# Plain float32 in the second feed-forward product, decays and state sum in one instruction each, and another order

## The chip, the cores and the metric

The kernel runs on one core of one Trainium2 chip. The metric is device time in microseconds (us) of one execution. The engines are PE (TensorE: matmuls, with its weight loads shown as PEld), DVE (VectorE), ACT (ScalarE), POOL (GpSimd) and SP (SyncE), which only issues transfers here. Each engine works through its own instructions in order; semaphores tie the engines to each other.

## The reference

Three layers, one after the other, all in float32.

```python
for t in range(S):                      # B, H, S, D = 4, 8, 768, 40
    y[:, :, t] = r_t @ state
    Sa = state @ a_t
    state = state * w_t - outer(Sa, b_t) + outer(v_t, k_t)
x = y.transpose(0, 2, 1, 3).reshape(B, S, 320)

h = relu(x @ w_in)                      # 320 -> 1024
conv = sum(conv_w[k] * h shifted by k - 1 tokens for k in 0, 1, 2)
x = (h * sigmoid(conv)) @ w_out         # 1024 -> 320

# four causal attention heads of 64 as experts, the best two of four mixed per token
```

The first layer is a recurrence over 768 tokens. The second is the feed-forward part; `w_out` is its second product. The third is attention over each of the four sequences.

## The kernel before, in words

**Recurrence.** The 768 tokens are cut into NT = 12 steps of 64, each into NC = 2 chunks of 32. `prep(n)` builds for a step what doesn't need the state: running products of the decays w (P) and their inverses (Q), k and b times Q (L297), a times P (L301), small products of the two (L313), a triangular inverse T. `chain(k)` carries the state from chunk to chunk: X (L448), the solved part (L464), the state's change as 16 products (L477), the sum with the old state (L496) and its decay (L498). `post(k)` gives the outputs y, multiplies by P (L549) and writes them to a scratch in memory.

The tile `a` holds two heads, in partitions 0 to 39 and 64 to 103, and two places for each. `load_a` puts head 0 into place 0 and head 1 into place 1; the free rows (64 to 95 of place 0, 0 to 31 of place 1) later receive F, the masked products of a and k (L319, L323). So the decays times a are two instructions of 40 partitions x 1024, one for each place (L299 to L302).

The 16 products of L477 fill the first 320 columns of two PSUM banks, four blocks of 80 in each. The state sum is therefore one instruction for each bank (L490 to L496).

**Feed-forward.** `ff()` makes one stage for each step and each of four pairs of 128-row blocks of h: 48 stages, and two more for what lags (LAG = 2). A stage does 16 first products (L683, 8 passes x 2 blocks), takes h out of PSUM (L693), and `gate` works it on: two ACT copies times conv_w (L645), four DVE instructions for the other taps (L649), the sigmoid (L652), times h on POOL (L654). Then the result g is split in two: `gh`, rounded to the fp32r format (L657, ACT), and `gl`, what is left (L660, POOL). Two stages later the second product takes them (L714): for each of two blocks and two halves of 128 tokens three fp32r products, gh x wh, gh x wl, gl x wh. The weights w_out are split in the same way at the start (L606 to L608). The last token is a small product of its own at the end (L728 to L733). `cv`, `h`, `gh` and `gl` have two buffers each, the loaded input `xd` one.

**Attention.** `proj`, `weigh`, `scale`, `turn`, `values` and `result` work through blocks of 128 queries; plain float32 products appear there in `values` (L944), and transposes in `turn` (L921).

**Order.** The parts are generators, merged by due times into one program. `in_order` then reads the table ORDER: for each engine a text of pairs (skip, size), each of which takes the next instructions of that engine, `size` of them, after `skip` of those still left. So the order on every engine is written out in full, and the engine waits wherever the next instruction in this order is not ready.

Of the kernel before, what the change touches and what calls it, by code (L numbers as in the profile page):

```python
# [8 lines left out]
F32 = mybir.dt.float32  # L9
# [34 lines left out]
def paced(g, start, span):  # L44

    for f in g:
# [11 lines left out]
        "Wg0k8A04-0C4kg04-0y4-0i8-0K8-1e80w-1y4-0a4-1u6M8wg08og0oAg-0UgY4w4Y2U4-2y6U8-2ii0Ego-1i40M-0y4k4-2G4g40A88I804"
        "8w0444cgYg04-0y4gg-0i8-2ma-0i8-264-2a2-264-0i40-02-1240gk80gA8-3644w04-2y6sg4gQg4w-1i204-1240w-0y40g8g-02444sw"
        "g8w88404Ygc4k4048804-0-4-0W404-0Ok-164-0O4-2S408gwwo-1S4wg-1C2wg0w8w-0s40g-064-084-062sg-2e404-2a6-0S4-1-40gMg"  # L60
        "-1y2-1u40w-0i8-128-0S40M4g8404cwk4sg-0egc8-0S4-0O4sg-0u4-0C4-0uc-2me-0K4-0eE-0K804-1u604-0C404-0yg-3O4-1240w-3"
        "e8-12g0w-2i80w-1O48g0wQ40wM8E40g4gU8-26agw04k4-1u2c4MgogUg0484-0q404-0m4-2ya04-0i8-2m2-0i4-2a8-0C8-168-0y4-1S4"
        "-4mc0w-0Cg-1Cg-3m40w-2S2-024-2U80w-4A4-2i40w-1O2-3-48g0wQ40wM8-0m8E40g-0244g04cw04ggogMg-0C4-0qc-2i404-0m4-06g"
        "04-02k-1mk0ww8-028-3Sc-06g0wQg0w-2q4-2mc4g-26g04-283-2e3-223g4-2130w48A84w-1f404-0M4-0P44gkg04-0f40k-0340g-034"
        "0wx4F8Zg-0j8-0r8-0D4-0L803-0I464033e09j30c76fc-22307gco4wco2r7o308scgai4g2w3g6m408ec8g082g062407O30gs3X3cc3394"
        "09M3cc03940c9g09e2-1A2kg0bo407-0P20624-1V2j8225cU805s3048g08cg-0r40cOc04K423056304240k430ch83b6402h401g4348432"
        "06a302m40143a404a36433d3v303a4y3a4w3a482e8C3g2I3e204C3ac04u7g604o3a202g8A408G2v8N3y4m30gv3630423023403C425x475"
        "02ec0594e80994g492i405d8944504u8egt80594k609l452j4548404134201ak34024401640376c4340854eo540554a4d40553c352h4q4"
        "0553i458rga4f8w2f405ncw40554y254Jkj8a605q4j4b8h4u408m2c393v4j406l4d4037343g304y344-003c488-04608aoq2a4w2a4s124"
        "s306e484a8j3850863z8h3t3063403w3c408m404g20cA248V40465Acr404a524s3o4068508g35404120184l8Ck845309m8540554e254i4"  # L70
        "t4055e05kci205ik04450454a805g456f405a4fo05r4j4a4j205a4d4g405io5305n6346406320j7k047234843172028405dg0514d61364"
        "420192gc021202h434d202130314012802240e",
    "Activation":
        "-0Z1-1m1110131012104a1l111411104f1j101110331514101219151312101f15161g1012111a11103210272e1g1f111d1a10111b1a1w1"
        "1101g101l102f111j1e1f1e101m111g1i2o211j1m1l102h111i1h1g1h1k1g21101h1e301l1d202k1h211g1b1a1g1037281731171i46101"
        "7111013342311161b1049101c11151c111b1a10111014201b1d1b2310122c101110181s1c1511121110112025122311101211141312111"
        "612161114321117121011101c13101310142g1i101g1f13101e101b1221101110151016172c1917201a1032103f2b2a2r192p404120181"
        "f121118101b101e1n241m1n1m10162a121b1a1018101d13101510141617101i161B16181e1110221028402q13103i1l1j181h221118102"
        "a10192211101k101j1i1h101h1v1g12251610151m15141G10171i1110211410421c184o4026131011101f1g12111013101211102l102n1"
        "41g10112610161e1a151a13181n1317132j11204d1b1d1c1b1r10112314131210131m11202c15101b131025261e1014111b29101218101"  # L80
        "6111b28101814171042101l101f2e10121e1c20411315111k1110181h42103410141211101713141813181g131e18171u161b4a2716142"
        "j1h161310141d1w101e151c101a104m11202m121f1116102b1t1b24101419102614281a1e1910171b101628101o17181410151n151g1h4"
        "g1w16102t11201q1r1q13103110111C201217101110161a1n1e10131210232g13181e28161b16171018151m101620151f151f2u1f10212"
        "a201k1A1k102112111f2p1f111e11201j1k101k1i101s1h2120131j1311201r1g101f1j1h1f1h1f1h1i2j1i1o1k1n2u30261E1D1610151"
        "815102513151310121720151810141726101a2937101a1619471015181517101a1614152013161015121522131210111h10122521161a1"
        "2112f101e1220121112141310121011291410131610121312101b1011131712161210161011141A101413101s101E12202f12102715112"
        "01C131413102214111210221110411021102622211316102411121023191310111015141214121015101115161112181228221011181j1"
        "3161015162b151029101a1815103a171011102314101911121011132013102210131220251l15132620241210141113202311121310221"
        "1101210131112101225131013111215101125121413161015161i151a1210111b24121316101316131c171510151410361510111213111"
        "0171b121e11101c101d13401410142013142312151011131029111416101510131110141013101f1210111011181617131710321316101"  # L90
        "214121025182130141113141210141011121d1110151415141014201113101210111320132013141310141015201710111012104110121"
        "0111312102420111413102520211410211011107",
    "DVE":
        "0821112111211121112111511131211101j211i2m1o1n1o1n1r102l11101m101m101g1l101i101h101h101g10as101-00141Z101Y102W1"
        "n1V1X12101U1l1T1l1W1V1Y1X1-011-001-011-00112011101k101j1n1j1m101F101k108310a113111211202v102w131c2m1f1j1i131h1"
        "0121011101p1o103p101p101n102r101q1B1q1A1q1j1s111r111q111p101o2r5u1r1t1r1s1r1u1r2310121011101l1w401v101v101u1t1"
        "u1t1u1t1i1s2012101m111i102l1g2i1g101g101g1f11102b101c201b1018102610151014121c12101513101210211011101p20g412131"
        "6121510161410454815101514a91514163215121810112024101413301211203k101j101i201h105d102510121012102a1810262011202"
        "g101f101l102j111n12101210121012101120151032101q102o1r2m111011101t101h101o101n101m1l103e104a1019106n102l10112w1"
        "11m102k101211121112111211121115111312111A121110221q1u1q101n103k11101p107k101j101g101f1075101310211l101k1153121"  # L100
        "31211841211201c151t131s132q131p1051107f207c10261015101410161022131011402m10121k1311131113111311151115111312112"
        "0111018101210211011108i101h102f101e101d102410131021103810171012201112113o1210121012101210121012101112112012111"
        "01a101110211p1n1s221112111k111i1110ae10551c1014101310271620112i111h111n111311131h141114111411171115102d1015102"
        "11011102110111j101i101h101g101i101h301g101g109910161716102n102l1s121r10111u111N1110131013102G10111011101110141"
        "0121043102n101m111011101l207e101d101c101c1039101810171016104h22201e2013102i101h3l202j23105j1h1i1h101l1j1k1j102"
        "6201518151025132012161j162h16101f101617162h1019101f1e3617161c1b101519151c15101435101410122312201610241210111c1"
        "610151418221011101a1013111023111211101g3311121310211m112u102b1I2G1H151G1F131j1D101i101h1110131112111t502210111"
        "021103435212023152032101c12102610171e171d151c141612161g1210171d101c12151c111b2811171211151a3f111e20241f1c1e1c4"
        "61b541c341c1027141610311025121415141013111019111617212210111a11121017201c3311102m1n1m10141k341j121i321h2410131"
        "11014321310121015323024321026321012111c30111321101115121b112924231n131o1n101m1l381510141h111g271f171e171119231"  # L110
        "017121320281612161512202916141012152f14101d27101f1a1e2t3c2011101c2a1v1b1a20191q191p19221822161217121022151i121"
# [32 lines left out]
class Kernel:  # L144
# [1027 lines left out]
```

## Time and profile before

| | us |
|---|---|
| median of 3 runs | 866.12 (865.93 to 870.81) |
| the profiled execution | 866.72 |
| its span, first to last instruction | 864.9 |
| PE busy | 726.0 (84%) |
| DVE busy | 681.5 (79%) |
| ACT busy | 576.8 (67%) |
| POOL busy | 370.2 (43%) |
| mean granted clock of PE | 0.931 |

Busy times are unions: two matmuls that lie over each other count once, and a matmul's record is longer than the time until the next may start. The recurrence ends near 525 us, the feed-forward part near 632, and attention runs from about 540 to the end. Shares of the whole span mix these stretches, so the rows below are taken by stretch or by line.

### The profile page before, as it was taken

The page shows a single profiled execution, that of the slowest core. Times are in us where ns is not written, and L with a number is a line of the kernel's source. Part 1 is how long each engine was busy: PE and PEld are TensorE (multiplying, and loading weights), DVE is VectorE, ACT ScalarE, POOL GpSimd, SP SyncE. Part 2 cuts the span into 40 slices and gives each one's busy share as a digit, 9 for nine tenths or more (in the row PEclk, how much of TensorE's full clock was granted, in tenths as well). Part 3 has the DMA queues.
Part 4 walks back from the last instruction along what each step waited for, and adds up shares of the span by engine and source line. Part 5 has one row for each costly group of instructions (what it writes and reads, how often), then busy time and mean ns, then how long its engine had stood idle before and what let it go on. Part 6 is the DMA issues. An engine that isn't in the chain of part 4 may idle for free. (4 is left out here: it accounts for less than half of the span.)

```text
span 864.9 us, 31373 instructions
## 1 busy us (share of the span) xinstructions
PE 726.0 (84%) x13080; PEld 639.9 (74%) x13080; DVE 681.5 (79%) x1541; ACT 576.8 (67%) x1359; POOL 370.2 (43%) x419
## 2 busy tenths in 40 slices
PE   1366658989978998988898897888999999999997
PEld 1255547878877877877797786887888888888876
DVE  6996968899989999999979854776667776877764
ACT  1274747677675785866676885689777665676665
POOL 6233463524424233153143437567543454442652
PEclk9997568599999897997979999999999999999999
DMA  5445576556656556565645444301010101110001
GB/s 134 109 114 134 139 162 157 119 111 158 141 137 134 130 120 129 134 126 132 152 101 144 109 100 127 87 20 30 16 50 36 48 16 33 38 39 17 16 17 39
DMA packets 143488, 81.17 MB, mean 94 GB/s; under 512 B 113858, under 2 KB 127042, under 8 KB 142386
## 3 DMA queue, kind: packets, MB, share of 16 engines
q1 hardware_dynamic: 138450, 74.34, 35.7%
q0 software_dynamic: 4896, 4.83, 2.7%
q8 instruction: 103, 1.69, 0.8%
q14 instruction: 39, 0.32, 0.1%
HBM read 51.63 MB, written 11.80 MB: 73 GB/s over the span
## 5 line engine op out<-in xcount | busy, mean ns | idle before, releaser
L907 POOL TENSOR_TENSOR A<-A,rs 128x128 f32<-128x128 f32 (+5 forms) x96 | 88.5, 943 | 102.1 <-DVE rs L905 79.3
L649 DVE SCALAR_TENSOR_TENSOR cv<-h,cw,cv 128x256 f32<-128x256 f32 (+1 forms) x192 | 104.0, 571 | 15.6 <-ACT cv L645 14.7
L714 PE MATMUL ps<-wout,gh 128*128 128x320 f32 x384 | 100.0, 332 | 4.0 <-ACT yt L741 4.0
L654 POOL TENSOR_TENSOR cv<-cv,h 128x512 f32<-128x512 f32 (+1 forms) x48 | 59.8, 1250 | 95.0 <-ACT cv L652 80.4
L683 PE MATMUL ps<-xh,win 128*128 128x256 f32 x384 | 94.2, 303 | 5.9 <-ACT hc L699 5.1
L683 PE MATMUL ps<-xl,win 128*128 128x256 f32 x384 | 93.6, 298 | 4.0 <-POOL xl L632 3.9
L660 POOL TENSOR_TENSOR gl<-cv,gh 128x512 fp32r<-128x512 f32 x48 | 59.8, 1249 | 52.6 <-ACT gh L657 37.2
L892 ACT ACTIVATE A<-ps,nm 128x128 f32<-128x128 f32 (+5 forms) x96 | 60.7, 633 | 27.8 <-DVE nm L890 23.2
L683 PEld LDWEIGHTS ps<-xh,win 128*128 128x128 f32 x384 | 69.2, 199 | 9.6 <-ACT hc L699 6.8
L683 PEld LDWEIGHTS ps<-xl,win 128*128 128x128 f32 x384 | 69.7, 200 | 5.5 <-POOL xl L632 4.8
L714 PEld LDWEIGHTS ps<-wout,gh 128*128 128x128 f32 x384 | 66.5, 196 | 7.2 <-ACT yt L741 5.0
L890 DVE TENSOR_REDUCE nm<-ps 128x1 f32<-128x128 f32 (+5 forms) x96 | 58.5, 620 | 15.7 <-PE ps L888 14.8
L714 PE MATMUL ps<-wout,gl 128*128 128x320 f32 x192 | 61.3, 320 | 2.5 <-POOL gl L660 2.5
L255 PE MATMUL ps<-kb,a 40*32 40x64 f32 x1536 | 32.3, 242 | 34.6 <-DVE kb L297 28.4
L255 PEld LDWEIGHTS ps<-kb,a 40*32 40x32 f32 x1536 | 27.7, 122 | 38.4 <-issue 17.5
L319 POOL TENSOR_TENSOR F<-F,cst 128x256 f32<-128x256 f32 x24 | 19.5, 813 | 83.6 <-DVE F L318 67.8
L831 PE MATMUL ps<-x,wqk 128*128 128x384 f32 x256 | 53.7, 347 | 0.9 <-DVE lg L825 0.9
L921 PE MATMUL ps<-cid,A 128*128 128x128 f32 x336 | 51.2, 276 | 1.8 <-DVE AT L924 0.9
L255 PE MATMUL ps<-RB,LB 104*40 104x32 f32 (+1 forms) x1536 | 41.4, 213 | 13.5 <-DVE RB L535 7.2
L255 PEld LDWEIGHTS ps<-RB,LB 104*40 104x40 f32 (+1 forms) x1536 | 37.4, 130 | 18.4 <-DVE RB L535 8.7
L470 ACT ACTIVATE VZ<-ps 32x640 f32<-32x640 f32 x48 | 33.5, 697 | 24.5 <-PE ps L255 23.7
L885 PE MATMUL ps<-k,q 128*128 128x256 f32 (+3 forms) x128 | 45.4, 361 | 4.4 <-ACT A L892 4.0
(177 smaller groups left out, 2148.8 us busy)
## 6 DMA issues: line engine op xcount, KB each, us to landing
kb<-in_kb_e_dram SPq DMA_DIRECT2D x24, 320.0 KB
LB<-KB SPq DMA_DIRECT2D x48, 160.0 KB
LB<-S SPq DMA_DIRECT2D x46, 100.0 KB
a<-in_a_e_dram SPq DMA_DIRECT2D x24, 160.0 KB
RB<-in_rb_dram SPq DMA_DIRECT2D x48, 80.0 KB
VZ<-in_v_dram SPq DMA_DIRECT2D x96, 40.0 KB
SV<-in_v_dram SPq DMA_DIRECT2D x48, 80.0 KB
ra<-in_ra_dram SPq DMA_DIRECT2D x48, 80.0 KB
```

The costliest lines, as they stand in the source:

```text
L255: self.nc.tensor.matmul(*a, **k)
L649: nc.vector.scalar_tensor_tensor(c[:, dd], h[:, dd, :, k:k + nt], ws[dd][:, k:k + 1], c[:, dd], op0=ALU.mult, op1=ALU.add)
L654: nc.gpsimd.tensor_tensor(c, c, h[:, :, :, 1:1 + nt], op=ALU.mult)
L660: nc.gpsimd.tensor_tensor(gl, cv[:, :, :, :TOK], gh.bitcast(F32), op=ALU.subtract)
L683: nc.tensor.matmul(hp[:, dd], wt[:, 128 * d:128 * d + 128], x, start=k == 0, stop=k == 7)
L714: nc.tensor.matmul(self.ps[1][:, tb, :DM], x, wt, start=d == 0 and k == 0, stop=d == 7 and k == 2)
L831: nc.tensor.matmul(pp, self.wqk[:, wk, hl, 128 * m:128 * m + 128], x[:, xk], start=j == 0, stop=j == 7)
L885: nc.tensor.matmul(sp[:, c0:c1], q[:, ce, 128 * j:128 * j + 128], k[:, ce, c0:c1], start=True, stop=False)
L890: nc.vector.tensor_reduce(nm, sp[:, :nk], axis=AX.X, op=ALU.max, negate=True)
L892: nc.scalar.activation(A[:, :nk], sp[:, :nk], AF.Exp, bias=nm, accum_out=sums[:, e:e + 1])
L907: nc.gpsimd.tensor_tensor(A[:, :nk], A[:, :nk], rs[:, e:e + 1].to_broadcast([128, nk]), op=ALU.mult)
L921: nc.tensor.transpose(tp[:, m, e], As[e][:, 128 * (2 * g + m):128 * (2 * g + m) + 128], self.cid)
```

## The change

1. **Second product.** `wout` holds w_out in plain float32, `gate` writes one float32 tile `g` straight from the product with h on POOL, and each block of the second product is one float32 matmul instead of three fp32r ones. The splits of g (ACT, POOL), of w_out and of the last token are gone.
2. **Decays times a.** Both heads are loaded into place 0, one instruction of 104 partitions multiplies them, and a transfer within SBUF copies head 1 to place 1, where the chain reads it. The products of L313 read both heads from place 0.
3. **State sum.** The 16 products write blocks of 128 columns, which lets one instruction take both banks. The last chunk, whose new state nobody reads, leaves out its 16 products, sum and decay.
4. **Buffers.** `cv`, `h` and `g` have three, `xd` two. `wx`, the helper of the weights, has a tile of its own.
5. **Order.** The ORDER texts of all five engines are new. Counted out, PE's places 7720 instructions, 8136 before, and its largest skip is 560, 354 before.

```diff
@@ setup_a, load_a
+        nc.vector.memset(self.ps[0][32:64], 0.0)
...
-            self.nc.sync.dma_start(a[R[h], :, h].rearrange("p b u t -> p b (u t)"),
+            self.nc.sync.dma_start(a[R[h], :, 0].rearrange("p b u t -> p b (u t)"),
@@ prep
-                return self.bw.tile(shape, F32, tag=tag, name=name, bufs=1)
+                return self.bw.tile(shape, F32, tag=tag, name=name, bufs=1 + (tag == "xd"))
...
-        for al in range(2):
-            av = a[R[al], :, al]
-            nc.vector.tensor_tensor(av, av, P[R[al]].rearrange("p (u b) t -> p b u t", b=2), op=ALU.mult)
-            yield 0.22 + 0.02 * al
+        av = a[E, :, 0]
+        nc.vector.tensor_tensor(av, av, P[E].rearrange("p (u b) t -> p b u t", b=2), op=ALU.mult)
+        yield 0.22
+        nc.sync.dma_start(a[R[1], :, 1].rearrange("p b u t -> p b (u t)"), a[R[1], :, 0].rearrange("p b u t -> p b (u t)"))
+        yield 0.24
...
-                    self.mm(WF, FG[32 * q:32 * q + 32, u].rearrange("p x s -> p (x s)"), a[r, be, q % 2, u0 + u],
+                    self.mm(WF, FG[32 * q:32 * q + 32, u].rearrange("p x s -> p (x s)"), a[r, be, 0, u0 + u],
@@ chain
-        for p in range(NP):
+        more = k + 1 < NT * NC
+        cf = cu.rearrange("p h x -> p (h x)")
+        for p in range(NP if more else 0):
             for al in range(2):
-                self.mm(WD, cu[R[al], p // 4, 80 * (p % 4):80 * (p % 4) + 80], KB[:, u0 + p, al],
+                self.mm(WD, cf[R[al], 128 * p:128 * p + 80], KB[:, u0 + p, al],
...
-        for h in range(2):
-            ps = slice(4 * h, 4 * h + 4)
-            Dv = cu[E, h, :320].rearrange("p (m b d) -> p m b d", m=4, b=2)
-            if zero:
-                nc.vector.tensor_tensor(st(sN)[:, ps], Dv, qq[:, ps], op=ALU.mult)
-            else:
-                nc.vector.tensor_tensor(st(sN)[:, ps], Dv, st(sT)[:, ps], op=ALU.add)
-        if not zero:
+        Dv = cf[E].rearrange("p (m x) -> p m x", m=NP)[:, :, :80].rearrange("p m (b d) -> p m b d", b=2)
+        if zero:
+            nc.vector.tensor_tensor(st(sN), Dv, qq, op=ALU.mult)
+        elif more:
+            nc.vector.tensor_tensor(st(sN), Dv, st(sT), op=ALU.add)
             nc.vector.tensor_tensor(st(sN), st(sN), qq, op=ALU.mult)
@@ setup_b, weights_b
-        self.wout = cp.tile([128, 8, 2, DM], F32R, name="wout")
+        self.wout = cp.tile([128, 8, DM], F32, name="wout")
...
-            x = self.narrow("w_out", lambda w: w[d], DM)
-            self.split(self.wout[:, d, 0], self.wout[:, d, 1], x, nc.vector if LO and self.nn % LO == 0 else nc.gpsimd)
+            self.narrow("w_out", lambda w: w[d], DM, self.wout[:, d])
@@ gate
-            nc.gpsimd.tensor_tensor(c, c, h[:, :, :, 1:1 + nt], op=ALU.mult)
-            yield
-            gh = bw.tile([128, 2, B, TOK], F32R, name="gh", bufs=2)
-            nc.scalar.activation(gh, cv[:, :, :, :TOK], AF.Copy)
-            yield
-            gl = bw.tile([128, 2, B, TOK], F32R, name="gl", bufs=2)
-            nc.gpsimd.tensor_tensor(gl, cv[:, :, :, :TOK], gh.bitcast(F32), op=ALU.subtract)
+            g = bw.tile([128, 2, B, TOK], F32, name="g", bufs=3)
+            nc.gpsimd.tensor_tensor(g, c[:, :, :, :TOK], h[:, :, :, 1:1 + TOK], op=ALU.mult)
             if n == NT - 1:
-                self.split(gx[:, 2 * dp:2 * dp + 2, 0], gx[:, 2 * dp:2 * dp + 2, 1], cv[:, :, :, TOK])
-            pend.append((n, dp, gh, gl))
+                nc.gpsimd.tensor_tensor(gx[:, 2 * dp:2 * dp + 2], c[:, :, :, TOK], h[:, :, :, 1 + TOK], op=ALU.mult)
+            pend.append((n, dp, g))
@@ ff
-                        vh, vl = [g[:, dd].rearrange("p b t -> p (b t)")[:, 128 * tb:128 * tb + 128] for g in (gh, gl)]
-                        wh, wl = self.wout[:, d, 0], self.wout[:, d, 1]
-                        for k, (x, wt) in enumerate(((vh, wh), (vh, wl), (vl, wh))):
-                            nc.tensor.matmul(self.ps[1][:, tb, :DM], x, wt, start=d == 0 and k == 0, stop=d == 7 and k == 2)
+                        v = g[:, dd].rearrange("p b t -> p (b t)")[:, 128 * tb:128 * tb + 128]
+                        nc.tensor.matmul(self.ps[1][:, tb, :DM], v, self.wout[:, d], start=d == 0, stop=d == 7)
...
-        k = 0
         for d in range(8):
-            for a, b in ((0, 0), (1, 0), (0, 1)):
-                nc.tensor.matmul(xp, gx[:, d, a], self.wout[:, d, b], start=k == 0, stop=k == 23)
-                k += 1
+            nc.tensor.matmul(xp, gx[:, d], self.wout[:, d], start=d == 0, stop=d == 7)
```

## Rows read from the trace of the kernel before

**Rows 1.** Windows view: stretch, length, PE, PEld, DVE, ACT, POOL busy us, PEclk, DMA.

```profile
0.00:50.00 50.00, 15.31 (x470) 12.94 (x474) 39.73 (x95) 9.93 (x24) 20.84 (x34) 1.00 0.48 119
...
125.00:525.00 400.00, 350.46 (x8773) 311.91 (x8775) 350.23 (x681) 284.97 (x619) 149.33 (x155) 0.90 0.56 128
525.00:632.00 107.00, 92.53 (x706) 84.95 (x706) 69.43 (x151) 82.36 (x191) 67.30 (x73) 1.00 0.21 52
632.00:864.90 232.90, 222.25 (x1885) 190.68 (x1883) 164.83 (x483) 153.32 (x426) 99.15 (x118) 1.00 0.10 32
```

**Rows 2.** Windows view, line L714 alone, the two stretches in which it runs.

```profile
125.00:525.00 400.00, 70.98 (x352) 55.24 (x352) 0.90 0.56 128
525.00:632.00 107.00, 39.98 (x224) 33.55 (x224) 1.00 0.21 52
```

**Rows 3.** Groups by line and form, ACT and POOL: busy us, mean ns | idle.

```profile
L657 ACT ACTIVATE gh<-cv 128x512 fp32r<-128x512 f32 x48 | 29.8, 627 | 8.2 <-POOL cv L654 5.0 <-PE ps L714 3.0
...
L660 POOL TENSOR_TENSOR gl<-cv,gh 128x512 fp32r<-128x512 f32 x48 | 59.8, 1249 | 52.6 <-ACT gh L657 37.2 <-issue 7.7 <-PE ps L259 3.5
```

**Rows 4.** Groups by line and form on DVE.

```profile
L649 DVE SCALAR_TENSOR_TENSOR cv<-h,cw,cv 128x256 f32<-128x256 f32 x176 | 96.0, 573 | 15.0 <-ACT cv L645 14.2
...
L301 DVE TENSOR_TENSOR a<-a,P 40x1024 f32<-40x1024 f32 x24 | 30.9, 1288 | 0.4
...
L297 DVE TENSOR_TENSOR kb<-kb,Q 104x1024 f32<-104x1024 f32 x23 | 28.2, 1261 | 0.9 <-DMA kb<-in_kb_e_dram 0.8
...
L496 DVE TENSOR_TENSOR sT<-ps,sT 104x320 f32<-104x320 f32 x46 | 21.6, 485 | 8.7 <-PE ps L255 6.7 <-ACT U L488 1.7
...
L498 DVE TENSOR_TENSOR sT<-sT,q 104x640 f32<-104x640 f32 x23 | 21.4, 928 | 0.1
```

**Rows 5.** Single lines on DVE: duration in ns min/median/max, first and last start.

```profile
L649 DVE SCALAR_TENSOR_TENSOR cv<-h,cw,cv x192: 380/478/1911, 147.7 to 625.3; 128x256 f32<-128x256 f32 x176, 128x260 f32<-128x260 f32 x16
...
L498 DVE TENSOR_TENSOR sT<-sT,q x23: 771/818/1926, 78.9 to 521.1; 104x640 f32<-104x640 f32 x23
...
L535 DVE TENSOR_TENSOR RB<-ps,cst x48: 669/689/696, 73.5 to 523.7; 64x512 f32<-64x512 f32 x48
```

**Rows 6.** Timeline near 568 us, POOL and DVE: start, length, instructions.

```profile
568.01 1.20 POOL L654 TENSOR_TENSOR cv<-cv,h 128x512 f32<-128x512 f32 x1 [1.75 <-issue]
...
568.32 1.57 DVE L649 SCALAR_TENSOR_TENSOR cv<-h,cw,cv 128x256 f32<-128x256 f32 x2 [1.59 <-ACT cv L645]
```

**Rows 7.** Timeline of PE near 604 us; the three lines between are L714 too.

```profile
604.13 0.46 PE L714 MATMUL ps<-wout,gh 128*128 128x320 f32 x2
...
605.01 0.31 PE L714 MATMUL ps<-wout,gh 128*128 128x320 f32 x1
```

**Rows 8.** Groups by line and form: PE's transposes and plain products, PEld's loads.

```profile
L921 PE MATMUL ps<-cid,A 128*128 128x128 f32 x336 | 51.2, 276 | 1.8 <-DVE AT L924 0.9 <-DVE x L573 0.4 <-ACT AT L926 0.4
...
L944 PE MATMUL ps<-AT,v 128*64 128x128 f32 x672 | 42.7, 277 | 1.1 <-ACT AT L926 1.0
...
L921 PEld LDWEIGHTS ps<-cid,A 128*128 128x128 f32 x336 | 37.7, 140 | 6.6 <-issue 2.6 <-POOL A L907 0.9 <-ACT AT L926 0.7
```

**Rows 9.** Timeline of PE near 300 us, and line L259 by itself.

```profile
300.43 0.52 PE L259 MATMUL ps<-cst,sT 104*104 104x104 f32 x4
...
L259 PE MATMUL ps<-cst,sT x184: 249/253/416, 56.8 to 518.6; 104*104 104x104 f32 x184
```

**Rows 10.** DMA issues: count, KB each, median us to landing.

```profile
xd<-xs POOLq DMA_DIRECT2D x24, 128.0 KB, 4.9
```

**Rows 11.** Timeline of DVE in the first step.

```profile
12.53 1.22 DVE L301 TENSOR_TENSOR a<-a,P 40x1024 f32<-40x1024 f32 x1
...
14.44 1.22 DVE L301 TENSOR_TENSOR a<-a,P 40x1024 f32<-40x1024 f32 x1
...
20.81 0.44 DVE L318 STREAM_TRANSPOSE F<-ps 128x256 f32<-128x256 f32 x1
```

**Rows 12.** Who waited for whom: us in total, times, longest.

```profile
PE ps L255 <- DVE kb L297: 28.4, 4, 16.9
```

More of the change, by code (lines that the diff above doesn't have):

```diff
@@ L58 @@
[L58 to L62, printed above, removed]
@@ new lines @@
+        "C8-1u8-0y4Ug-02g-0W40www0wEg-0a4owU40g8go8U808-0u80gw4M8-028-2G80wwo0gwg0g-124Q4-0-c-0i80gU40w4gQ8M4gw04-1i404"
+        "Ig84gg04Ig-0y404-0O8-1i8-0i4-1-4-0i4-02g-06g-028-1e4-0y4-424-1a80w-02g-12g0w-2i8-4O40w-1Og8g-0m4-3Kc0w-0i8-0a4"
+        "-0O8-4G40ggg0g4gYggw04c4-06gsg04-0q4-2a404-0Cc04-1a4-128-1G80w-0yg-1yg0w-2O80w-2ic0w-1O4-3-408go0gQ40wM8-0m8E4"
+        "-2m4-0i40g4gUg04cw-06g04-0G8og-0q404-0m4-2e404-2a4-0y4-02E-0yc0w-0O8-02g-12g0w-2ic-4K40w-1Oc-3-48g0g-0640g-3a4"
+        "-0i8-0S8-0a40M-0eg-0-g0oE48w04-0C4-2q8kg04-264-0i4-02w-068-0C8-0240w-0K4-3y40wAg-0Ggw4U4-2i80w-4e4-1O88g-1y40w"
@@ new lines @@
+        "3303g43303730434n37434B203-05304u1k204840cU3X48wo30882e3i3e48ah38304a304z8h394p36706s38408g208I2044c04R4Fcw465"
+        "04B3x406450hg35605p453m458vg05q404m8540554e254i4t4055e05k4ia041401ek4504e454055aa4f405jo0554a4n6f405a4d4g405io"
+        "08a434f6063207340332ak340334033a051401ag02b205a664339203dc024403b613440158034402220c",
+    "Activation":
+        "-0R1-1d1-1w111013101211103a1l111411104f1j1011103320131219151012111f151h1012111b1110111i1c1011291g201f1e10111p1"
+        "t1d1c102f1011101d111c1l1h1c2d1i201e201h1f1g1f10111c1j1c2i1h1d1c301b1j1b2i1h211g121h1a191d2e101829181j101i20191"
+        "61f1e16201810151815141j3y1j201a1N14131a13101612101m12111l151114101b181918101b261b1a101119101C141316152e2O1e171"
+        "d1w105m1U1m2n1m102112102u481120171b1F1A2C1B10141y1m1M101-021110142918191810161A101-0819152017112016103n2o1n105"
+        "110121s2f1s171q1X12111016101l1c10211h1013261720151X10181j101j132g11151013101b14102m1W1q1m2o1n1m103211101t2u1t1"
+        "812111017101z1012212915132K1811152014101j1413151g1h151f2032102F1n1X121m2n1m104110121f1r171q1t1s1120161n1m1S101"
+        "2201110171r122520142W101j17132i1g203w10211o131V101m2n1m1031101v201u221f1025101V1E2A10151y2110381t101g122617152"
+        "01y1Q1420151-0316111034104112111h2B1i1h1310171e121110251V131b12102327162c161d1c1b1m1a1714191U142g10121g101d161"
+        "31b101o102W1q2m4021202t1s2t1210251o1B2T101B1z2013141-0311101u142938171B101a1-091015201v271v101t111025102z1D1-0"
+        "71z2B1z2042101G201G1F181028101z1e1J101W1I2-061I201P121110111L211L2K1-01111P101-071024331120141K1210311F1A301z1"
+        "B121R1031102u2v121t1110111s1u201t1F121s1021202q1p1r1p2A101w1r1v1t1s1r1q1l1w1q3r1q1y1q1026101m2w1m1n151l151l151"
+        "7103t1g321f13121d103f2a1n1a38101910182m182019101914181c1l1918101310183722101i11101d171611171521161d16112g14121"
+        "412101n111412101c13211411101220161210111011101b1m1110121021101622201116101214111210231118121011101310121012101"
+        "41015161119151a14201710191k141710191810151b1014111018251017102a171011101410141019111015111411101310241210121p1"
+        "210162410111215201213121013141310231112131022111012101321101214151014112a121913121310141210121k121413141013121"
+        "71016121412101422101b14132021103224101110171b1022101f1b1012371210131410141312141312152210131a11101411121410221"
+        "11410222e101110191711171017101110231611151220251126211014111314121014101f1112111510141514101420111012201113101"
+        "42210151320141015202115101210111012101311121012101110232110131210242210141310222021104",
@@ new lines @@
+    "DVE":
+        "0211062111211121112111211102120111i201h101g111j1l1k1l1k1o1k101m101h1l101j1k1j101j10cs101-0010141Y101X102V1m1X1"
+        "U12101T1k1S1k1V1U1X1W1-001Z1-001Z112011101j101J1i101l1h101j101i10a110611m111l105t1D161m1n1i101k1011103r104r1M1"
+        "s1r1K1x1q1w101v101u101w101v101u4x4G1x1A1x1z1x101w101v2B101E1u1D1z1C101B101A1C1B1C1A2B1A1s1z441v141u141u1t301u1"
+        "01r101q101n1l1m1l1n101n101l101k1p10121011102c1d1c101x101w101a191a1012101110231q131p10121n1011102e101d101h101e1"
+        "01g101f101x101w101a1019104r101q101p101o10111r11104210211011101x105211102p101o1B1n1A101z1p2x1T111011101P101M101"
+        "L108e10561015104l101k1153111l11121112111211121114102t101s1q101p12101y10111o2011101p101o101n107f10751014101s101"
+        "r101l201n111m114n101211121012101210121014101s101r103B102z1x1r2v102s11101i101h10c81017106l2q101n111m111l1120221"
+        "1121110821110171r1p1q1p1011101p202t11101r101o101n109d10461015104q1r1q10111o111i101h103210121012101210121014101"
+        "a101r11101q1p101o102B1z102y111m201t101M101M101K101J102i10691018107l2011531211308210271r1p121o101n10111o2110111"
+        "0f9103a1b1a131913103153112j111i121112181c18111a121112111b10121t1r11101q1p102y101x1v211011101l201O101L101L101J1"
+        "06e10471016103n101Q101P1l101L111K112032101210121h10121012101F101E1012103K101w1J1w1H203M11101L1K208G101F101E101"
+        "D1091121120111s4032101s101r1p202p4t101s1q202C1D1C201D1B1C1B101110151x251w2527103r121r1q131p121011101819182k181"
+        "j181g181f181017401a1b1a20241c1a1410192018172932101116101118111715212210142n1220163421103112112019301r1s121q121"
+        "011171m101l8216201510151012131026331021101c221b10171110241b131a10191410141e101d111c10142b231a171e3713161310161"
+        "h1d1i1d1f1g1f1d1e38101c4e20141c1d10131017141610311013151014121410131220181617241110211a1119121017121t1u101s5b3"
+        "21o112m151014121i131h121g131012153012131012101532131210243210263210112c30142124191210121311141730122l1n1l1m1l2"
+        "21k321j101i121h14172216101522101116231513201310211b201a10131i101h161g122i201h17111a101s301d1e2d2a1c101b301a322"
+        "6121i22101g13101412151i121h241210111510151i101h12101f12161011141t101s201g281d1e1d321c101b111a10191a10181622101"
+        "f301216131014121110131d15111b211520232012111i1k151810171g171d311c101b101a3b1a241910131422101216101510141210173"
+        "310122013143014102214321024301110163210112014301116101522101112144026231510121021407",
@@ new lines @@
+    "Pool":
+        "l101-001310261f151a181a191817131a1319101213121110131041202p211031102f101110111c10311l2c101d1b21121a19103610261"
+        "0131014101311122012111022351430111312111014122a1b192011102233121b1c1a204240111b11101a191810123j12101i1h1012111"
+        "d10141220111h2i1h102233121n121m1l101k111014125m2n1m101120166j3i181c1b1a10221120141h1g2f14601310123610211023101"
+        "61110161021101110122110131210312011103243121514151013107110122081105110312021101110122440141310131210231214202"
+        "31011101110131210311041105110711011105",
@@ new lines @@
+    "SP":
+        "11310231210121j111h101a191a1917302715101413103p1o1f11101S1110161N1014181a2k1j11121026222110132d1026101715101f1"
+        "l27143B141a1A141024101g1f1e2f1e1910171610141j1e29182d1b191a191p1810181c171j2i1b1d18171b1a19181718371s1q1016371"
+        "0251j142g101b2v1t161514101210152015141a1716171011201215141w1615121021181n121110162314131f1i2j1i1f1b2v1t1c1b111"
+        "041101829181426221110262714131s131p131210241k23141E1C1h1g1331101a1018121120181a1918111j24171611121810231x1v121"
+        "3221d11181p101a1m171D181j1i1y1712112d101b111031201829181e1120152a10181y111613151v10111211171610152413182B1z1h2"
+        "e1810341810111710241a181918101712101d1c151a102611151q101112101n101p1324131h131A1d1f1z131d102a19101312111016171"
+        "613181712101511141a391517113021102n131k161413141g131f102v1a191r10182t1012111018251a10121110151b101a13122312231"
+        "413221n1o192m1617102h1x1y131f11301a18222024181310441226143613141910121011101n1o1n12112g1f121e3q1916111o1512114"
+        "01g2011102R1S1R1Q14231011231211101g10242d2c11202g1411121110121110161016111022102e2d211011101810651322104110211"
+        "210241310311013104310411021101210c",
```

94 lines of the change are left out of this document (18 added, 76 removed).

## The prediction

> **What bounds the kernel now.** I began with the busy time of the engines by stretches [rows 1]. The reader is to see that no engine is the bound everywhere. From 0 to 50 us only DVE works in earnest (39.7 of 50). From 125 to 525, the steady part of the recurrence, PE and DVE are level: 350.5 and 350.2 of 400, 88% each. From 525 to 632, where the feed-forward part finishes while attention starts, PE has 92.5 of 107 and ACT 82.4, 77%. After 632 PE has 222.3 of 232.9, 95%: that is what "full" looks like in this measure. POOL is nowhere above 63%.
>
> The groups by line come next. The second product is L714, with 576 records, one for each of its three partial products; 352 lie before 525 us and 224 after [rows 2]. The split parts cost 48 copies on ACT (0.627 us) and 48 subtractions on POOL (1.249) [rows 3]. The decays times a are 24 DVE instructions, the state sum 46 [rows 4].
>
> Last, the durations of single DVE lines. Here the reader is to see a spread that the group means hide: L649 has a median of 478 ns, a mean of about 571 (rows 4 give 573 for 176 of its 192) and a maximum of 1911; L498 has 818 and 1926. L535, of similar size, which reads PSUM and only one full operand from SBUF, stays between 669 and 696 [rows 5]. A stretched pair of L649 begins at 568.32 and takes 1.57 us for 2, while POOL's L654, which reads two SBUF tensors, runs from 568.01 to 569.21 [rows 6]. So POOL's work over SBUF data lengthens DVE's: an engine far from full still costs the fullest one time.
>
> **The change, part by part.**
>
> 1. *PE, second product.* Six of the present products start between 604.13 and 605.01 [rows 7]: 0.147 us each, 0.46 ns a column, and 0.44 for the three of a block (one 128-row slice of g by one 128-token half). Plain float32 needs two records for each product: L921 transposes 336 tiles with 336 records, L944 multiplies the same 336 tiles with 672 [rows 8]. A plain pass over 104 columns: four of L259 in a row take 0.52 us from the first start to the last end, and one alone 0.25 at least, so they start some 0.09 apart, 0.86 ns a column [rows 9]. So a pass over 320 columns is 0.275 and a block 0.55: 0.11 more, and 192 blocks make +21 us of PE, +12.9 before 525 and +8.2 after. Bounds: at the pace of the present form a block would be 2 x 0.147 = 0.29 and the sum -28. If the weight loads (140 ns for a plain one of 128 columns [rows 8]) were not hidden, a block would be 0.83 and the sum +75. I take 0.55: the transposes move plain float32 through the same array, and PE's busy time shows loads of L921 lying beside its matmuls (140 ns beside 276 ns). The last token's products go from 24 x 0.147 to 8 x 0.55, +0.9; the last recurrence step loses 16 small products, under 1.
>
>    The Trainium skill ("Perfetto Trace Analysis", Engine Utilization) puts the array's output for FP32_LOW_HIGH at one half. Read as the cost of a whole product, that would be two times 0.147 for a block, and PE would gain 28 us; a mechanism like that is rival 4. "FP8 and Floating Point Precision" (TensorE Precision Notes) speaks against the change: true float32 is four passes. Rows 8 and 9 agree with the four: two records, each at half pace.
>
> 2. *ACT and POOL, no split.* ACT loses 29.8 and POOL 59.8 [rows 3], and on top what the eight weight tiles cost, which I don't price. By the records of L714 224/576 = 39% of it lies after 525 [rows 2]: 11.6 of ACT and 23.3 of POOL. From the sigmoid to the product, the chain of a stage loses 0.63 + 1.25 = 1.9 us.
>
> 3. *DVE, decays.* 24 x 1.288 become 12 instructions of 104 rows; L297 does 104 x 1024 in 1.261 [rows 4]. So -15.8: three quarters of it, -12, in the steady part (nine of the twelve steps), the rest before.
>
> 4. *DVE, state sum.* The trace shows no PSUM sum of 640. L496 has 485 ns for 320 [rows 4], L535 a median of 689 for 512 [rows 5]: 1.06 ns an element, so about 825. Ends: 689 (nearest smaller) and 970 (two of today's). 46 x 0.485 become 22 x 0.825, and L498 and the sum are dropped in the last step: -4.2 - 0.9 = -5, of which I count 2.5 in the steady part, since one sum must now wait for all sixteen products where the first half could start early.
>
> 5. *DVE, less stretching.* L649 spends 176 x (573 - 478) ns = 16.7 us, L498 23 x (928 - 818) = 2.5 above their medians [rows 4, 5]. L660 is half of POOL's work in a feed-forward stage, and it goes. From nothing to all 19 of these could go with it, and the small DVE instructions that read SBUF are stretched too; I take 12, half of it in the steady part.
>    The Trainium skill ("SBUF — State Buffer", Who interferes with whom) says that a DVE instruction with two SBUF inputs and a GpSimd instruction that reads SBUF exclude each other for a whole instruction. Rows 5 and 6 agree. By that rule alone each of the 48 subtractions can hold up one DVE instruction for up to its own 1.25 us, 60 in all, and more than my 12 could go.
>
> 6. *The new copy of a.* Twelve transfers within SBUF, 160 KB each. The trace gives no landing time for a transfer within SBUF; one of 128 KB from POOL's queue takes 4.9 [rows 10]. In SP's queue it waits for the decays, and the F transfers (L323) behind it now wait for it to land, because F goes into the rows that it reads. Between them lie 64 small products, two transposes and two masks on three engines, and in the first step already F's first transpose starts 20.81, 5.1 after the last decay ended [rows 11]. So I count nothing; the worst end is 12 x 4.9 = 59 if each were waited out in full.
>
> 7. *Three buffers instead of two* for h, cv and g, and two for xd: below nothing, not priced. *The order:* the text for PE now reaches up to 560 places ahead in the program, 354 before; the products of the feed-forward part are left behind longer. No row prices that; I leave it at nothing and give it a rival.
>
> **The sum.** The profiled execution took 866.7 us (span 864.9 and 1.8 around it), 0.6 above the median of 866.1.
> - 0 to 125: the first matmuls wait for L297 (28.4 us of PE's idle time in four waits [rows 12]), and L297 stands behind both decays, 12.53 and 14.44 [rows 11]: one of 1.22 goes from the path. Two later ones count half, 1.2. Together -2.
> - 125 to 525: DVE loses 12 + 2.5 + 6 = 20.5, PE gains 12.9. Two engines at 88% hold each other up. Six tenths of DVE's relief appear, -12. That leaves PE at 363 of 388, 94%, just under the 95% of the last stretch.
> - 525 to 632: PE goes from 92.5 to about 101.5, ACT from 82 to 71, and each stage's chain is 1.9 us shorter. PE's idle 14.5 us shrink to a few: -3.
> - After 632: untouched, 0.
> Sum -17, 849.7, as a median **849 us**.
>
> **The rivals.**
> 1. *PE takes over as the bound (slower).* If PE's records already stand for a full engine in the steady part, the +12.9, +8.2 and +0.9 all land on the path and DVE's relief only becomes idle time. With the -2 at the start: 866 + 22 - 2 = 886. It decides once PE's share from 125 to 525 would pass some 95%. For it: PE's clock is 0.90 there [rows 1], so part of it runs at the lower of the two levels (1.2 and 2.4 GHz), where a pass takes twice as long. Against it: 12% idle today. Chance 0.13.
> 2. *A trade.* DVE's -12 in the steady part is just met by PE's +12.9, the tail keeps its length, the start gives 2: 864. For it: the two engines are level, and a fixed order can only follow the slower. Chance 0.18.
> 3. *The order uses it all.* The deeper reach lets the recurrence run with little feed-forward work in the way; DVE's 20.5 and 8 instead of 3 in the tail appear: 866 - 2 - 20.5 - 8 = 835. Chance 0.10.
> 4. *Plain float32 is cheaper than I hold*, two passes at full pace: PE loses 28 us, and half of that shows on top of the forecast, 835. Rows 9 speak against it. Chance 0.03.
>
> **How the numbers follow.** The forecast has 0.56. A measurement of this kernel tells about 1% (8.7 us) from no change. Faster by over 1%: forecast, rivals 3 and 4, 0.56 + 0.10 + 0.03 = 0.69. Within 1%: rival 2, 0.18. Slower: rival 1, 0.13. The range goes from 830 (rival 3 and a little for the unpriced buffers) to 869 (rival 2 and the spread around it); outside lie rival 1 and some of rivals 3 and 4, about 0.18.
>
> **What the profile will show.** Right, if L714 has 384 records, close to 0.275 us apart, ACT and POOL have lost 30 and 60 us or more, L649's mean has come nearer its median, DVE is some 33 us lower in total, and the last stretch is as long as now. Wrong, if PE's share in the steady part goes to 95% and the recurrence ends no earlier (rivals 1 and 2), if SP or the F transfers wait for the new copy, or if the records of L714 follow each other at 0.147.

## The result, and the profile after

The changed kernel takes **844.1 us** (median of four runs, 842.8 to 847.0), the one before 866.6 beside it: ratio 0.9735, 95% interval [0.9695, 0.9775]. That is 22.5 us less. The forecast was 849 with a range of 830 to 869. The profiled execution took 843.7 us, span 842.0.

The profile page of the changed kernel, busy time of the engines:

```profile
PE 728.2 (86%) x12848; PEld 614.5 (73%) x12848; DVE 644.8 (77%) x1500; ACT 545.7 (65%) x1299; POOL 297.1 (35%) x367
```

Its stretches, cut as in [rows 1]; the last one ends with the span:

```profile
0.00:50.00 50.00, 16.24 (x528) 13.90 (x528) 38.83 (x95) 10.31 (x26) 21.56 (x35) 1.00 0.51 130
50.00:125.00 75.00, 52.54 (x1346) 45.27 (x1340) 57.62 (x127) 46.12 (x99) 27.13 (x35) 0.73 0.60 145
125.00:525.00 400.00, 357.15 (x8639) 300.25 (x8636) 336.67 (x671) 273.95 (x609) 113.79 (x136) 0.94 0.57 134
525.00:632.00 107.00, 102.13 (x637) 82.50 (x636) 62.88 (x177) 76.82 (x189) 44.63 (x61) 1.00 0.21 57
632.00:842.00 210.00, 200.10 (x1721) 172.53 (x1719) 148.81 (x432) 138.54 (x377) 89.97 (x102) 1.00 0.09 29
```

From 125 to 525 PE went from 350.5 to 357.2 and DVE from 350.2 to 336.7 in the same 400 us, and POOL from 149.3 to 113.8, with more of the program done by 525. PE's granted clock over these 400 us went from 0.90 to 0.94; the forecast has no term for that.

Groups on the lines of [rows 4] (by line and form):

```profile
L647 DVE SCALAR_TENSOR_TENSOR cv<-h,cw,cv 128x256 f32<-128x256 f32 x176 | 91.8, 543 | 27.4 <-ACT cv L643 21.2 <-ACT hc L692 4.5 <-POOL F L319 0.5
L496 DVE TENSOR_TENSOR sT<-ps,sT 104x640 f32<-104x640 f32 x22 | 18.1, 821 | 2.6 <-PE ps L254 2.6
L299 DVE TENSOR_TENSOR a<-a,P 104x1024 f32<-104x1024 f32 x12 | 15.6, 1300 | 0.0
```

and single lines with min/median/max and first and last start, as [rows 5]:

```profile
L647 DVE SCALAR_TENSOR_TENSOR cv<-h,cw,cv x192: 385/482/1608, 127.7 to 600.5; 128x256 f32<-128x256 f32 x176, 128x260 f32<-128x260 f32 x16
...
L497 DVE TENSOR_TENSOR sT<-sT,q x22: 784/818/1817, 73.6 to 504.3; 104x640 f32<-104x640 f32 x22
...
L705 PE MATMUL ps<-wout,g x384: 430/432/903, 137.7 to 610.4; 128*128 128x320 f32 x192
```

The second product before ended with this group:

```profile
L714 PE MATMUL ps<-wout,gl x192: 302/309/636, 161.7 to 631.2; 128*128 128x320 f32 x192
```

The last decay of the state starts at 504.3 instead of 521.1 [rows 5], the gate's last DVE instruction at 600.5 instead of 625.3, the last record of the second product at 610.4 instead of 631.2. So 17 us come out of the recurrence; the gate ends another 8 sooner, of which 4 are lost again before the product ends. From its last record to the end of the span are 231.6 us, 233.7 before.

The pace of the plain product, on the timeline, start and length first:

```profile
565.94 2.32 PE L705 MATMUL ps<-wout,g 128*128 128x320 f32 x8
```

Eight records in 2.32 us, of which the last is shown with 0.43: seven steps in 1.89 us, 0.27 each, 0.54 a block. DVE lost 36.7 us in all, ACT 31.1, POOL 73, and PE's busy time rose by 2 only, though blocks became longer. Busy PE time counts the overlapping tails of matmuls, so the pace, not the busy time, gives the price.

At the start the first matmul comes 1.4 us sooner, and now waits for the decays:

```profile
15.50 3.73 PE L254 MATMUL ps<-kb,a 40*32 40x64 f32 x128 [15.50 <-DVE a L299]
```

Before it began at 16.89, behind kb. This is the new order, not the merged product: the first product with kb now stands ahead of the decays, and in the run below that has the decays apart again the first matmul starts at the same time:

```profile
15.49 0.42 PE L254 MATMUL ps<-kb,a 40*32 40x64 f32 x2 [15.49 <-DVE a L300]
```

There the rest of the 128 matmuls waits for the second decay and is through at 20.27; here all are through at 19.23.

### The profile page after: what moved, and what is told of

Read it like the earlier page. It is cut to its first block, busy times and chain, and to the rows that moved or that the text cites. A ratio compares the mean times of both kernels' runs of the same rounds, so it can differ in the third digit from the quotient of the medians.

```text
span 842.0 us, 30735 instructions
## 1 busy us (share of the span) xinstructions
PE 728.2 (86%) x12848; PEld 614.5 (73%) x12848; DVE 644.8 (77%) x1500; ACT 545.7 (65%) x1299; POOL 297.1 (35%) x367
## 4 chain that ended last, share of the span: by engine, by line
PE 45%; DVE 19%; ACT 12%; DMA 10%; SPq 6%; issue 5%; POOL 2%; DVEq 0%; ACTq 0%; POOLq 0%
PE ps L254 11%; PE ps L676 6%; PE ps L705 5%; PE ps L932 4%; PE ps L909 3%; PE ps L819 3%; PE ps L810 2%; PE ps L873 2%; PE ps L258 2%; DVE cv L647 2%; PE ps L874 2%; PE ps L948 2%; ACT A L880 2%; DMA w<-in_w_e_dram 2%; DMA xs<-xe 2%
## 5 line engine op out<-in xcount | busy, mean ns | idle before, releaser
L647 DVE SCALAR_TENSOR_TENSOR cv<-h,cw,cv 128x256 f32<-128x256 f32 (+1 forms) x192 | 99.6, 540 | 28.1 <-ACT cv L643 21.4
L705 PE MATMUL ps<-wout,g 128*128 128x320 f32 x384 | 116.5, 446 | 1.0 <-ACT yt L729 0.6
L653 POOL TENSOR_TENSOR g<-cv,h 128x512 f32<-128x512 f32 x48 | 59.6, 1244 | 126.7 <-ACT cv L650 116.2
L676 PE MATMUL ps<-xh,win 128*128 128x256 f32 x384 | 97.2, 312 | 2.2 <-issue 1.4
L705 PEld LDWEIGHTS ps<-wout,g 128*128 128x128 f32 x384 | 70.6, 194 | 26.3 <-issue 2.5
L254 PEld LDWEIGHTS ps<-RB,LB 104*40 104x40 f32 (+1 forms) x1536 | 37.1, 132 | 15.3 <-issue 6.7
L643 ACT ACTIVATE cv<-h,cw 128x256 f32<-128x256 f32 (+1 forms) x96 | 45.8, 504 | 0.3
L490 ACT ACTIVATE U<-VZ 32x320 f32<-32x320 f32 x96 | 44.9, 468 | 1.6
L650 ACT ACTIVATE cv<-cv 128x512 f32<-128x512 f32 (+1 forms) x48 | 30.2, 629 | 23.5 <-DVE cv L647 23.1
```

Source lines behind the costliest of these rows:

```text
L254: self.nc.tensor.matmul(*a, **k)
L643: nc.scalar.activation(c[:, dd], h[:, dd, :, :nt], AF.Copy, scale=ws[dd][:, 0:1])
L647: nc.vector.scalar_tensor_tensor(c[:, dd], h[:, dd, :, k:k + nt], ws[dd][:, k:k + 1], c[:, dd], op0=ALU.mult, op1=ALU.add)
L653: nc.gpsimd.tensor_tensor(g, c[:, :, :, :TOK], h[:, :, :, 1:1 + TOK], op=ALU.mult)
L676: nc.tensor.matmul(hp[:, dd], wt[:, 128 * d:128 * d + 128], x, start=k == 0, stop=k == 7)
L705: nc.tensor.matmul(self.ps[1][:, tb, :DM], v, self.wout[:, d], start=d == 0, stop=d == 7)
```

## Experiments

All edits are made to the changed kernel and keep its order: an instruction that is put back stands where its counterpart stands, or right behind the one that it reads. The runs are called e1 to e12. They were measured in three groups (e1 to e4, e5 to e8, e9 to e12), each with the kernel before beside it; ratios are against that one. The control, e9, is the changed kernel again, in the third group. So the changed kernel has two ratios, 0.9735 and 0.9704, with the intervals [0.9695, 0.9775] and [0.9651, 0.9758].

**Decays apart (e1).**

```diff
-        av = a[E, :, 0]
-        nc.vector.tensor_tensor(av, av, P[E]...)
-        nc.sync.dma_start(a[R[1], :, 1]..., a[R[1], :, 0]...)
+        for al in range(2):
+            av = a[R[al], :, al]
+            nc.vector.tensor_tensor(av, av, P[R[al]]...)
...
```

The loads and the products of L313 go back to the two places with it.

> The changed kernel (844.1) with its decays times a in two instructions each again and without the copy of a; everything else, the order too, as changed. DVE gets 12 x (2 x 1.29 - 1.30) = 15.4 us back. Theory (DVE and PE hold each other up in the steady part, about six tenths of DVE's relief shows): +8 to +11, 852 to 855. Rival (the gain came from the order and the buffers, not from DVE): 844 to 846. Second rival (the copy costs what the merging saves): 840 to 844.

844.1 us, ratio 0.9721 [0.9683, 0.9759]. DVE's total is up by 10 us, the time is not. Taken alone this leaves two readings: DVE has slack, or the copy costs what the merging saves.

**Sums apart**, twice (e2 and e12).

```diff
-        nc.vector.tensor_tensor(st(sN), Dv, st(sT), op=ALU.add)
+        for h in range(2):
+            nc.vector.tensor_tensor(st(sN)[:, ps], Dv, st(sT)[:, ps], op=ALU.add)
...
```

The 16 products fill columns of 80 again, as before.

> The changed kernel with its state sum in two instructions of 320 again, all else as changed. DVE gets 22 x (2 x 0.485 - 0.821) = 3.3 us back. Theory: +1 to +2.5, 845 to 847, near what can be told. Rival (the sum of 640 starts later than its first half could, which costs the recurrence): 840 to 843.

840.9 us, 0.9685 [0.9638, 0.9732].

> The changed kernel with its sums apart, against the control on the same chip: it measured 840.9 in another group where the changed kernel had 844.1 elsewhere. Theory (the first half of a sum starts while the second half's products run, which is worth more than 3.3 us of DVE): -1 to -4 against the control. Rival (chance): within 1 of the control or above it.

840.6 us, 0.9672 [0.9631, 0.9714], beside the control's 845.8 and 0.9704. That is 5.2 us by the medians and 2.8 by the ratios. Both measurements point to a few us less than the changed kernel, but the intervals overlap: merging the sums brings nothing that can be told, and may cost 3 us.

**The load of the old second product (e3).**

```diff
+            nc.scalar.activation(da, g, AF.Copy)
+            nc.gpsimd.tensor_tensor(dm, c[:, :, :, :TOK], g, op=ALU.subtract)
-                        nc.tensor.matmul(ps, v, self.wout[:, d], ...)
+                        for k in range(3):
+                            nc.tensor.matmul(ps, v, W[:, k, 0, :DM], ...)
...
```

The tile `g` is written in the fp32r format for it. The products read `g` as soon as POOL has written it and do not wait for the copy or the subtraction, so the longer way from the sigmoid to the product is not among what e3 puts back.

> The changed kernel with the load of the old second product: three single-pass products per block (0.44 us for 0.54), a copy on ACT and a two-operand subtraction on POOL per stage, their results unused; the products use other weights and leave the low parts out. PE loses 192 x 0.10 = 19 us, ACT gains 30, POOL 60. Theory (PE's loss shows by half, -8 to -10; the stretching of DVE and the longer chain cost +8 to +12): 842 to 848. Rival 1 (PE is the bound of the changed kernel): 825 to 832. Rival 2 (the split work was the main cost): 852 to 862.

860.5 us, 0.9900 [0.9869, 0.9931]: 14 to 17 us over the two ratios of the changed kernel. The second rival comes out. Its groups for the added work, on ACT and POOL:

```profile
L657 ACT ACTIVATE da<-g 128x512 bf16<-128x512 f32 x48 | 30.2, 629 | 28.6 <-POOL g L656 28.1
L658 POOL TENSOR_TENSOR dm<-cv,g 128x512 f32<-128x512 f32 x48 | 61.2, 1275 | 3.8
```

They are as long as the copy and the subtraction of the kernel before [rows 3]. Its engines:

```profile
PE 721.6 (84%) x13040; PEld 635.5 (74%) x13040; DVE 658.5 (76%) x1500; ACT 572.3 (66%) x1347; POOL 360.2 (42%) x415
```

**All the old work (e4): the edits of e1, e2 and e3 together.**

> All three at once: decays and sums apart, and the load of the old second product, in the changed kernel's order and buffers. What is left between it and the kernel before (866.6) is the order and the buffers. Theory (the work made the gain, the order is worth little): 858 to 866. Rival (the order and the buffers made it): 844 to 852.

867.0 us, 1.0009 [0.9972, 1.0046]: the kernel before, to within the interval. So beside the old work the order and the buffers bring nothing that can be told, and in the new order the work explains the gain. Not back are the splits of the eight weight tiles and of the last token, the last chunk's products, sum and decay, and the longer way to the product. That these savings and a cost of the new order cancel out is possible; the order alone was not run. The new work in the old order and buffers was not run either, so whether it would gain as much there is not shown. Taking decays and sums apart cost 6.4 us on top of the split load (866.96 against 860.54, same group), though each alone cost nothing.

**The two by two (e9, the control, and e10).**

> The changed kernel itself, as the control of this group: 842 to 846, ratio 0.970 to 0.976. All theories expect the same.

845.8 us, 0.9704 [0.9651, 0.9758].

> Decays and sums apart together, without the split load: beside the run with split load and both apart (866.96, against 860.54 with the split load alone) it makes a square of two by two. Theory (without the split load DVE has slack in the steady part, so its 18.7 us return at no cost; with it DVE is late and the same work cost +6.4): the same as the control, within 2 us. Rival (each merging is worth its part, and the two single runs missed it by chance): +6 or more against the control.

843.1 us, 0.9703 [0.9658, 0.9747], the control's ratio, with DVE busy 656.3 us against the control's 638.7. Without the split load the two mergings, copy included, are worth nothing; with it 6 us. The parts don't add up one by one. Read the other way, the split's removal is worth 24 us with decays and sums apart (e4 867.0, e10 843.1, in different groups), the whole gain, and 14 to 17 with them merged.

**The copy alone (e11).**

```diff
-        nc.sync.dma_start(a[R[1], :, 1]..., a[R[1], :, 0]...)
+        if n < 2:
+            nc.sync.dma_start(a[R[1], :, 1]..., a[R[1], :, 0]...)
```

> The changed kernel with the copy of a kept in the first two steps and left out in the other ten; what would be copied is left out of the result. Theory (the copy is hidden, 0): the same as the control, within 2 us. Rival (taking the decays apart also took the copy away, and its cost of 8 us or so hid what DVE lost): -6 or more against the control, 838 or less.

836.6 us, 0.9631 [0.9586, 0.9675], 9.2 below the control and below every other kernel here. Its interval overlaps the control's, but not that of the first measurement of the changed kernel, nor that of e1, which has no copy at all but the decays apart (0.9721 [0.9683, 0.9759]). This speaks for the rival: the copy is not hidden, ten transfers cost some 6 to 9 us, and that ate what the merged decays gave, some 8 between e1 and e11. In its profile the recurrence ends earlier: the last decay of the state starts at 489.7,

```profile
L498 DVE TENSOR_TENSOR sT<-sT,q x22: 805/817/1857, 73.8 to 489.7; 104x640 f32<-104x640 f32 x22
```

and in the control's at 505.6:

```profile
L497 DVE TENSOR_TENSOR sT<-sT,q x22: 782/818/1827, 75.1 to 505.6; 104x640 f32<-104x640 f32 x22
```

Which wait pays for it no line shows. PE waits 2.6 us for the F transfers behind the copy in the changed kernel and not at all here, but the waits differ as much between runs that have all the copies (3.1 in e7, none in e6). The issue alone takes time on SP; of the changed kernel:

```profile
L301 SPq DMA_DIRECT2D a<-a x12: 804/843/892, 16.2 to 468.7; - x12
```

The ten that e11 leaves out are 8.4 us in the queue through which all transfers of the recurrence go. That is of the size, but no more than a fit: whether the issue, the landing or the wait of the F transfers costs was not tried.

**The parts of the split load**, one at a time. First e5, the products of e3 without its copy and subtraction.

> The changed kernel (844.1) with three single-pass products per block instead of the plain one, and no split work on ACT and POOL; other weights, the low parts left out. PE loses 192 x 0.10 = 19 us. The split load together cost +16 (e3). Theory (PE's time shows by half): 833 to 837, so that ACT and POOL cost +24 to +27 in e3. Rival 1 (PE is the bound): 823 to 828. Rival 2 (PE's time has slack, or more products cost something of their own): 842 to 847.

846.1 us, 0.9711 [0.9662, 0.9761]. On its timeline eight records of the product take 1.33 us where eight plain ones took 2.32, and three of them make a block:

```profile
565.71 1.33 PE L706 MATMUL ps<-win,g 128*128 128x320 f32 x8
```

That is 0.146 each (1.33 less about 0.31 for the last, over seven), 0.44 a block. PE's busy time falls by 13 us:

```profile
PE 715.0 (85%) x13040; PEld 631.6 (75%) x13040; DVE 639.5 (76%) x1500; ACT 547.9 (65%) x1299; POOL 297.6 (35%) x367
```

The time does not fall, within some 6 us that the intervals leave: rival 2. Not all of the 19 us reach PE, though. PE's mean granted clock is 0.939 over the six runs of e5, 0.949 over the ten of the changed kernel, and its busy time shows 13. With that said, the plain product's extra 0.10 us a block is off the path, and PE is not the bound of the changed kernel before 632.

Then the subtraction (e6), a control for it (e7) and the copy (e8):

```diff
+            nc.gpsimd.tensor_tensor(dm, c[:, :, :, :TOK], g, op=ALU.subtract)      # e6
+            for _ in range(2):                                                     # e7
+                nc.gpsimd.memset(dm, 0.0)
+            nc.scalar.activation(da, g, AF.Copy)                                   # e8
```

> The changed kernel with one more POOL instruction per stage: a subtraction that reads two SBUF tensors of 512 and writes one that nobody uses; 48 x 1.25 = 60 us of POOL. Theory (what the split cost is DVE stretched by POOL's reads): +8 to +16, 852 to 860, with the mean of the gate's DVE instruction from 543 to 570 ns or more. Rival (it was ACT, or the longer chain): 843 to 847.

854.4 us, 0.9826 [0.9778, 0.9874], just clear of both intervals of the changed kernel: 8 to 11 us over its two ratios.

> The control of the run with POOL reads: two memsets of 512 per stage in the same place, about the same time on POOL, reading nothing. Theory (reading two tensors stretches DVE, being busy doesn't): 843 to 847 and the gate's DVE instruction at 540 to 550 ns. Rival (POOL's time in the queue is what costs): the same as the run with reads.

846.5 us, 0.9741 [0.9689, 0.9792], not to be told from the changed kernel. The page of the run whose added POOL work reads two tensors:

```profile
PE 728.7 (86%) x12848; PEld 612.4 (72%) x12848; DVE 665.4 (78%) x1500; ACT 547.8 (64%) x1299; POOL 358.4 (42%) x415
```

and of the one whose added work only writes:

```profile
PE 727.7 (86%) x12848; PEld 613.0 (72%) x12848; DVE 644.0 (76%) x1500; ACT 547.0 (64%) x1299; POOL 347.0 (41%) x463
```

DVE has the same 1500 instructions in both. With 61 us more of POOL reading it is busy 20.6 us longer than in the first profile of the changed kernel; with 50 us more of POOL writing, 0.8 less. Between executions of the same DVE work this total varies by some 6 us (644.8 in the first profile of the changed kernel, 638.7 in the control's), so 20 is well outside that and 0.8 is not. The same subtraction in e3 added 13.7 to 19.8, and in e4 19.9 over e10, so 14 to 27 us is what the runs allow. The gate's line carries part of it. In the run that reads:

```profile
L648 DVE SCALAR_TENSOR_TENSOR cv<-h,cw,cv 128x256 f32<-128x256 f32 x176 | 97.3, 573 | 23.9 <-ACT cv L644 19.1 <-ACT hc L694 3.2 <-POOL g L654 0.5
```

and in the one that writes:

```profile
L648 DVE SCALAR_TENSOR_TENSOR cv<-h,cw,cv 128x256 f32<-128x256 f32 x176 | 90.1, 533 | 30.2 <-ACT cv L644 24.4 <-ACT hc L695 4.6 <-POOL g L654 0.4
```

573 ns is what the kernel before had [rows 4]; e3 has 554. In these two profiled executions the spans are equal (850.3 and 850.2); that the readers cost time and the writers don't rests on six runs each, 849.6 to 858.3 and 842.4 to 852.0, whose ratios' intervals overlap a little.

> The changed kernel with one copy of g on ACT per stage, behind POOL's product, unused; 48 x 0.63 = 30 us of ACT. Theory (ACT has room everywhere but from 525 to 632, where it is at 72%): +1 to +4, 845 to 848. Rival (a copy that waits for POOL in ACT's queue holds up the recurrence's copies behind it): +8 or more, 852 and up.

850.2 us, 0.9787 [0.9735, 0.9839]: 4 to 7 us over the two ratios of the changed kernel, with overlapping intervals, so not settled. The waits show where it could come from:

```profile
ACT da L656 <- POOL g L655: 20.8, 21, 1.9
```

The copy itself is 30 us, and ACT stands idle for another 20.8 in front of it, while what is queued behind it waits too. Taken with e5 and e6 the sizes add up: 8 to 11 for POOL's subtraction, 4 to 7 for ACT's copy and nothing for the products, against 14 to 17 for e3.

## Why the prediction was right

The forecast was 5 us too high and its case, the likeliest, is the one that came: faster by over 1%, with the gain ahead of 632 and the last stretch about as long as before. The reasons held less well than the sum; that it came so close is in part luck, as two errors met.

- *Point 1, PE.* Right in size: 0.54 us a block against the 0.55 of the forecast, two records 0.27 apart; three single-pass products measured 0.44. So +19 us for 192 blocks where +21 stood. What the step made of it was too heavy: it let PE's gain hold back four tenths of DVE's relief. Giving the 19 us back (e5) changed nothing that can be told, and PE stands at 89% from 125 to 525, not at the 94% of the sum. Rivals 1 and 2 fall with that, and rival 4 with the pace. By the Trainium skill ("FP8 and Floating Point Precision", TensorE Precision Notes) true float32 is four passes; the pace agrees: two records, each 0.27 us where a single-pass one takes 0.146.
- *Point 2, ACT and POOL.* The totals fell by 31.1 and 73, where 29.8 and 59.8 stood and the weight tiles were not priced. The step that failed is what they were worth: the sum gave the shorter chain 3 us, in the stretch from 525 to 632 alone. The split load is worth 14 to 17 without any longer chain (e3), by far the largest part of the gain, and it shows in the recurrence too: its last decay starts at 517.2 with the split load, at 504.3 and 505.6 without.
- *Point 5, stretching.* The mechanism is shown by e6 and its control: POOL's subtraction takes 14 to 27 us from DVE where 12 stood, 20.6 of them in e6 (the rows allowed 19 and some for small instructions), and 8 to 11 us of time. The rule of the Trainium skill that was weighed there ("SBUF — State Buffer", Who interferes with whom), that a DVE instruction with two SBUF inputs and a GpSimd one that reads SBUF exclude each other, agrees with this trace in kind; in e6 61 us of POOL cost DVE 20.6, a third.
- *Points 3 and 4, decays and sum.* Right as busy time: 24 x 1.288 became 12 x 1.300, -15.3 (-15.8 stood), and one sum took 821 ns where 825 was estimated. Wrong as time. They carried 14.5 of the 20.5 us on which the -12 of the steady part rested, and together they brought nothing that can be told (e10 against the control).
- *Point 6, the copy.* "I count nothing" is the term that failed: ten of the twelve copies cost some 6 to 9 us (e11), close to what the merged decays would have given alone (e1 against e11).
- *Point 7, the order.* Nothing stood, and beside the old work nothing came: all of it in the new order and buffers runs as the kernel before (e4). Rival 3's 835 was not reached; what the order gives together with the new work is not shown.
- *The start.* The term of -2 was one merged decay on the path and two counted half. The first decay of the state starts 5.3 us sooner (73.6, 78.9 before), but with the decays apart as well (73.1 in e1), so the merging is not the reason.

The two errors: most of the -12 was ascribed to the merging and nothing to its copy, while the split's removal was put at less than half of what it gave (3.6 of the steady part's 12 and the 3 after it).

What stays open: what bounds the steady part now. PE is 89% busy there, DVE 84%, and taking 19 us from PE or giving 18.7 to DVE (e10, less the copy) moves nothing that can be told. Whether ACT's copy makes the rest of the split's cost, beyond POOL's reads, is not settled either. Nor is PE's clock: over all its runs the granted clock averages 0.929 in the kernel before and 0.949 in the changed one, and of 44 runs of the kernel before, the 20 with less than 0.93 took 870.3 us on average, the other 24 866.3. So some us of the gain may have come with the clock. It isn't the whole: e6 has 0.948 and is 8 to 11 us slower, e5 has 0.939 and is not. The run with two copies leaves out what the result needs; of those that don't, the sums apart measured lowest, not by more than chance could give.

## What to carry to other kernels

Price an edit by the engines that it disturbs, not only by the one that it relieves: here 48 POOL subtractions that nobody waited for cost 8 to 11 us, and 19 us of PE, by pace, nothing that could be told. A merging that needs a transfer to lay out its result must be priced with that transfer, even if nobody is seen waiting for it. Where two edits relieve the same engine, measure the square of two by two: the two mergings brought 6 us beside the old split and nothing without it.

## What the runs showed that was not expected

One SP issue of the copy takes 0.84 us of SP's queue, though the page counts no busy time for it. And PE's granted clock goes with the form of the second product: with three single-pass products it averages 0.929 (before), 0.938 (e3), 0.936 (e4) and 0.939 (e5), with the plain one 0.946 to 0.954 in each of the other ten. What PE did otherwise just before its clock fell was not compared.
